# Attention with 16 queries and 2048 keys on one core: engine loops, whole V units, and a wait of QK on V

## The chip, the cores and the metric

The kernel runs on one core of a Trainium2 chip. The metric is device time in microseconds (us) of one execution. Executions of one kernel mostly agree within 0.1%, so differences of 1 us can be told apart here if enough runs stand beside each other.

## The reference

```
B, H, Sq, Skv, Dh = 8, 16, 16, 2048, 256        # q, k, v in bf16
scores = einsum('bhqd,bhkd->bhqk', q, k) * Dh ** -0.5
attn   = softmax(scores, axis=-1)
out    = einsum('bhqk,bhkd->bhqd', attn, v)
```

There are 128 heads. K and V are 134 MB each and every byte is used once, while a head has 16 queries only: the kernel is a stream of 268 MB from HBM with some arithmetic beside it.

## The kernel before

A *unit* is four heads: 8192 rows of K or V, laid out as 128 partitions x 64 rows x 256, so a partition's share of a unit is one contiguous run of 32 KB. A *block* g is the two units 2g (even) and 2g+1 (odd). There are 16 blocks. K and V each have one SBUF buffer for an even and one for an odd unit. A *packet* is one contiguous run that one of the 16 DMA engines moves: 32 KB when a unit is loaded whole, 16 KB when it comes in halves.

For a block, DVE transposes K in eight pieces (`kt`), PE multiplies (`qk`), DVE takes the maximum, ACT the exponential, DVE transposes P (`pt`, `px`), and PE multiplies by V (`pv`) one block later. A *hardware loop* lets an engine repeat one stretch of instructions for every block; an *unrolled* stream has every block written out. Only PE loops here. The parts:

```python
def v_parts(u):                                   # pieces in which a V unit is loaded
    return vparts.get(u, [HT, HT] if u % 2 else [NT])       # NT = 64 rows, HT = 32
# V of block g may be loaded when PV of block g-1 is done:
#   deps = ... [("pv", g - 1, 1)] if g else ...
# K of block g, unit e, when the last transpose of block g-1, unit e, is done: [("kt", g - 1, e, 3)]

for g in range(G):                                # order of the loads in SP's queue
    for u in (2 * g, 2 * g + 1): k_load(u)
    if g:
        for u in (2 * g - 2, 2 * g - 1): v_load(u)

def qk(g, e, h):
    j_qk[g, e, h] = J("pe", "qk", ..., [("kt", g, e, 2 * h + 1), ("qwb", g, e) if h == 0 else None,
                                        ("exp", g - 1, h) if g and e == 0 else None])
def pv(g, h):                                     # first half needs only half of the odd unit
    j_pv[g, h] = J("pe", "pv", ..., [("px", g, h), ...]
                   + (j_v[2 * g] + j_v[2 * g + 1][:1] if h == 0 else j_v[2 * g + 1][1:]))

qk_block(0)                                       # PE's order; a hardware loop over blocks on PE alone
for g in range(1, last):
    qk_block(g); pv(g - 1, 0); pv(g - 1, 1)
# ... cut: the last block, ACT's and DVE's orders (unrolled), stores on ACT's queue
```

## Time and profile before

The kernel before takes 640.6 us (median of 3 runs, 640.5 to 640.74). These are lines of its page. In the first part: engine, busy us, share of the span, instructions. In the 40 slices a digit is a tenth of busy time. In the DMA part: packets, MB, share of 16 engines.

```profile
span 639.2 us, 4824 instructions
PE 489.1 (77%) x2176; PEld 166.7 (26%) x1680; DVE 427.8 (67%) x372; ACT 99.1 (16%) x208; POOL 4.2 (1%) x7
PEclk9979979799897999899898998997979989899899
DMA  9999999999999999999999999999999999999996
...
q1 hardware_dynamic: 13488, 269.51, 98.7%
q10 hardware_dynamic: 2288, 1.03, 0.6%
q8 instruction: 4, 0.07, 0.0%
q14 instruction: 6, 0.05, 0.0%
```

DMA is full in 39 of 40 slices, and no compute engine is near that. q1 is SP's queue (loads), q10 ACT's (stores), and the two instruction queues fetch program code through the same DMA engines. The window view of one steady block, from one landing of even K to the next (length, busy time of each engine, granted clock, DMA share, GB/s):

```profile
233.63:272.69 39.06, 30.36 (x124) 9.53 (x93) 26.49 (x23) 5.66 (x12) 0.00 (x0) 0.91 1.01 431
```

The Trainium skill, "DMA: Bandwidth & Descriptors", section Specifications, gives 435 GB/s as the fabric ceiling. The 431 GB/s here lie just under it. The timeline of the kernel before around the even K that landed at 233.6 us (start, length, engine, line, operation):

```profile
218.98 13.97 PE L171 MATMUL O_ps<-VB,PT 128*128 128x512 bf16 x64 [1.27 <-DMA VB<-in_v_dram]
...
232.98 1.28 SPq L229 DMA_DIRECT2D VB<-in_v_dram  x3
...
233.63 8.89 DVE L126 STREAM_TRANSPOSE KB<-KN 128x2048 f32<-128x2048 f32 x4 [9.38 <-DMA KN<-in_k_dram]
```

I call the landing of even K on its slowest DMA engine T (233.60 here; DVE starts 0.03 us later). PV ends at T-0.6 and the next V loads are issued at once. The odd K ahead of them in the queue keeps the DMA engines busy until T+9.7 (its 4 MB last 9.7 us), so the issue has ample time. In 3 of 14 blocks PV starts at half clock (*cold*: its first seven or eight matmuls come every 427 ns instead of every 215), as in the block after this one, where it takes 15.66 us instead of 13.97:

```profile
258.14 15.66 PE L171 MATMUL O_ps<-VB,PT 128*128 128x512 bf16 x64 [2.11 <-DMA VB<-in_v_dram]
```

There V is issued at T+1.2 (273.83, with T at 272.67), still early.

### The profile page before, as it was taken

The page shows a single profiled execution, that of the slowest core. Times are in us where ns is not written, and L with a number is a line of the kernel's source. Part 1 is how long each engine was busy: PE and PEld are TensorE (multiplying, and loading weights), DVE is VectorE, ACT ScalarE, POOL GpSimd, SP SyncE. Part 2 cuts the span into 40 slices and gives each one's busy share as a digit, 9 for nine tenths or more (in the row PEclk, how much of TensorE's full clock was granted, in tenths as well). Part 3 has the DMA queues.
Part 4 walks back from the last instruction along what each step waited for, and adds up shares of the span by engine and source line. Part 5 has one row for each costly group of instructions (what it writes and reads, how often), then busy time and mean ns, then how long its engine had stood idle before and what let it go on. Part 6 is the DMA issues. An engine that isn't in the chain of part 4 may idle for free.

```text
span 639.2 us, 4824 instructions
## 1 busy us (share of the span) xinstructions
PE 489.1 (77%) x2176; PEld 166.7 (26%) x1680; DVE 427.8 (67%) x372; ACT 99.1 (16%) x208; POOL 4.2 (1%) x7
## 2 busy tenths in 40 slices
PE   0857879676896768868689686787967878676998
PEld 0111313123131221312214122131311313122287
DVE  4879386693857949387492965938669395693861
ACT  2121112030120301212011120211203012030010
POOL 2000000000000000000000000000000000000000
PEclk9979979799897999899898998997979989899899
DMA  9999999999999999999999999999999999999996
GB/s 322 428 431 426 432 433 441 435 427 428 421 438 429 431 429 429 437 439 425 437 414 443 431 429 431 425 430 433 437 441 425 432 417 440 429 429 430 421 427 258
DMA packets 15786, 270.65 MB, mean 423 GB/s; under 512 B 1824, under 2 KB 4128, under 8 KB 4640
## 3 DMA queue, kind: packets, MB, share of 16 engines
q1 hardware_dynamic: 13488, 269.51, 98.7%
q10 hardware_dynamic: 2288, 1.03, 0.6%
q8 instruction: 4, 0.07, 0.0%
q14 instruction: 6, 0.05, 0.0%
HBM read 269.48 MB, written 1.05 MB: 423 GB/s over the span
## 4 chain that ended last, share of the span: by engine, by line
DMA 67%; DVE 25%; PE 7%; issue 1%; SPq 0%; DVEq 0%
DMA KN<-in_k_dram 67%; DVE KB L126 23%; PE O_ps L177 4%; PE S_ps L143 1%; PE S_ps L131 1%; DVE negm L148 0%; DVE PC L157 0%; SPq L110 0%; DVE PT L163 0%; DVE O_fin L323 0%; DVE O_fin L313 0%; DVE rab L292 0%; DVE rinv L291 0%; DVEq L410 0%; DVE ltot L289 0%
## 5 line engine op out<-in xcount | busy, mean ns | idle before, releaser
L126 DVE STREAM_TRANSPOSE KB<-KN 128x2048 f32<-128x2048 f32 x128 | 284.6, 2281 | 159.7 <-DMA KN<-in_k_dram 139.3
L143 PE MATMUL S_ps<-KB,QW 128*128 128x512 bf16 x528 | 213.1, 413 | 125.2 <-DVE KB L126 125.2
L171 PE MATMUL O_ps<-VB,PT 128*128 128x512 bf16 x896 | 200.7, 386 | 22.2 <-DMA VB<-in_v_dram 22.2
L131 PE MATMUL S_ps<-KB,QW 128*128 128x512 bf16 x496 | 203.9, 411 | 0.0
L143 PEld LDWEIGHTS S_ps<-KB,QW 128*128 128x128 bf16 x528 | 54.0, 103 | 327.7 <-issue 239.4
L171 PEld LDWEIGHTS O_ps<-VB,PT 128*128 128x128 bf16 x896 | 87.9, 99 | 138.0 <-issue 38.6
L119 ACT ACTIVATE QW<-QT 32x128 bf16<-32x128 bf16 x128 | 53.9, 421 | 320.5 <-PE S_ps L131 312.8
L163 DVE COPY PT<-PC 32x1024 bf16<-32x1024 bf16 x128 | 53.3, 416 | 4.3 <-PE O_ps L177 2.6
L157 DVE STREAM_TRANSPOSE PC<-P_sb 128x1024 bf16<-128x1024 bf16 x32 | 37.9, 1223 | 19.8 <-ACT P_sb L152 19.8
L152 ACT ACTIVATE P_sb<-S_ps,negm 128x1024 bf16<-128x1024 f32 x32 | 35.4, 1110 | 36.3 <-DVE negm L148 26.7
L148 DVE TENSOR_REDUCE negm<-S_ps 128x1 f32<-128x2048 f32 x16 | 36.7, 2292 | 4.6 <-PE S_ps L131 4.1
L308 ACT ACTIVATE O_tmp<-O_ps,rab 128x256 f32<-128x256 f32 x15 | 7.1, 474 | 157.9 <-PE O_ps L171 157.1
L177 PE MATMUL O_ps<-KN,PT 128*128 128x256 bf16 x128 | 14.4, 273 | 0.0
L177 PE MATMUL O_ps<-VB,PT 128*128 128x256 bf16 x128 | 14.1, 273 | 0.1
L177 PEld LDWEIGHTS O_ps<-VB,PT 128*128 128x128 bf16 x128 | 12.4, 98 | 2.0 <-DVE PT L163 0.6
L177 PEld LDWEIGHTS O_ps<-KN,PT 128*128 128x128 bf16 x128 | 12.4, 98 | 1.8 <-DMA KN<-in_v_dram 0.3
L323 DVE TENSOR_SCALAR O_fin<-O_ps,rab 128x256 bf16<-128x256 f32 x2 | 1.0, 483 | 11.5 <-PE O_ps L177 11.5
L313 DVE SCALAR_TENSOR_TENSOR O_fin<-O_ps,rab,O_tmp 128x256 bf16<-128x256 f32 x15 | 6.7, 448 | 1.8 <-issue 1.8
L152 ACT ACTIVATION_READ_ACCUMULATOR P_sb<-S_ps,negm 128x1 f32 x32 | 6.3, 196 | 0.0
L113 DVE STREAM_TRANSPOSE QT<-VB 128x2048 f32<-128x2048 f32 x1 | 2.3, 2311 | 5.5 <-DMA VB<-in_q_dram 5.5
L292 DVE TENSOR_SCALAR rab<-mask,rinv 128x2 f32<-128x2 f32 x16 | 3.7, 228 | 0.6
L190 POOL MEMSET PT<- 128x4096 f32 x1 | 3.5, 3512 | 0.0
(11 smaller groups left out, 7.8 us busy)
## 6 DMA issues: line engine op xcount, KB each, us to landing
KN<-in_k_dram SPq DMA_DIRECT2D x28, 4096.0 KB, 30.1
VB<-in_v_dram SPq DMA_DIRECT2D x32, 2048.0 KB, 26.5
VB<-in_v_dram SPq DMA_DIRECT2D x14, 4096.0 KB, 20.0
KN<-in_k_dram SPq DMA_DIRECT2D x8, 2048.0 KB, 15.3
KN<-in_v_dram SPq DMA_DIRECT2D x2, 2048.0 KB, 27.6
KN<-in_v_dram SPq DMA_DIRECT2D x2, 1024.0 KB, 23.1
KN<-in_v_dram SPq DMA_DIRECT2D x3, 512.0 KB, 25.8
VB<-in_q_dram SPq DMA_DIRECT2D x4, 256.0 KB, 4.4
```

Source lines behind the costliest of these rows:

```text
L119: ins = eng.activation(ap_of(dv, dv.offset + 32 * a + e, [[256, 4], [128, 2], [2, 16]]), ap_of(sv, sv.offset + 2 * (2 * g + e), [[64, 4], ...
L126: return eng.transpose(KBf[:, c % R_KB].rearrange("p t i -> p (t i)"), KNf[:, e].rearrange("p t i -> p (t i)")[:, n * c:n * c + n])
L131: return eng.add_instruction(mybir.InstMatmult(start_tensor_calc=start, stop_tensor_calc=stop, ldweights=False, tile_size=(128, 128), tile ...
L143: ins = mm(S_ps[:, 2 * h + c, :], QW[:, e, bp, :], rhs, start=(e == 0 and bp == 0), stop=(e == 1 and bp == 7))
L148: return eng.tensor_reduce(out=negm[:, g:g + 1], in_=S_ps[:].rearrange("p c n -> p (c n)"), axis=AX.X, op=ALU.max, negate=True)
L152: return eng.activation(P_sb[:, 1024 * h:1024 * h + 1024], S_ps[:, 2 * h:2 * h + 2, :].rearrange("p c n -> p (c n)"), ACTF.Exp, bias=negm[ ...
L157: return eng.transpose(PC[:, h].rearrange("p t x -> p (t x)"), P_sb[:, 1024 * h:1024 * h + 1024])
L163: ins = eng.tensor_copy(PT[pr, 32 * h:32 * h + 32, pr], PC[pr, h])
L171: ins = eng.matmul(O_ps[:, 0, :], PT[:, t, :], rhs, start=(t == 0), stop=(t == NT - 1))
L177: ins = eng.matmul(O_ps[:, bank, 0:D], PT[:, t, :], buf[:, t, :], start=(t == 0), stop=(t == NT - 1))
L308: j_ea[g] = J("act", "ea", lambda eng: eng.activation(O_tmp[:], src, ACTF.Copy, scale=rab[:, g, 0:1]), [("pv", g, 1) if g < last - 1 else ...
L313: j_eb[g] = J("dve", "eb", lambda eng: eng.scalar_tensor_tensor(out=O_fin[:, g % 2, :], in0=src, scalar=rab[:, g, 1:2], in1=O_tmp[:], op0= ...
```

## The change

It has three parts. First, DVE and ACT run as hardware loops of one block as PE does, with semaphore waits cut to what is needed; with that come one exp of 2048 instead of two of 1024, slices by register on ACT, and stores issued from SP's queue. Second, every odd V unit of blocks 0 to 13 is loaded in one piece, runs of 32 KB instead of two of 16 KB; PV then waits for all of it. Third, QK of the odd unit waits until the even V unit of the block ahead of it has landed, so that PV follows QK closely. The core of the diff, with cuts:

```diff
-        vparts = {NU - 2: [32, 32], NU - 4: [32, 32], NU - 1: [16, 16, 8, 8, 8, 4, 2, 2]}
+        vparts = {NU - 4: [32, 32], NU - 3: [32, 32], NU - 2: [32, 32], NU - 1: [16, 16, 8, 8, 8, 4, 2, 2]}
         def v_parts(u):
-            return vparts.get(u, [HT, HT] if u % 2 else [NT])
+            return vparts.get(u, [NT])
...
         for g in range(G):
             for u in (2 * g, 2 * g + 1):
                 k_load(u)
+            if g >= 3:
+                store("sp", g - 3)
             if g:
                 for u in (2 * g - 2, 2 * g - 1):
                     v_load(u)
...
-                              [("kt", g, e, 2 * h + 1), ("qwb", g, e) if h == 0 else None,
-                               ("exp", g - 1, h) if g and e == 0 else None])
+                              [("kt", g, e, 2 * h + 1), ("qwb", g) if e == 0 and h == 0 else None,
+                               j_v[2 * g - 2][0] if 0 < g < last and e == 1 and h == 0 else None,
+                               ("exp", g - 1) if g and e == 0 else None])
...
-                           [("px", g, h), ("eb", g - 1) if g and h == 0 else None]
-                           + (j_v[2 * g] + j_v[2 * g + 1][:1] if h == 0 else j_v[2 * g + 1][1:]))
+                           [("px", g, h), ("eb", g - 1) if g and h == 0 else None] + j_v[2 * g] + j_v[2 * g + 1])
...
-        emit_stream(nc.scalar, "act")
-        emit_stream(nc.vector, "dve")
+        emit_stream(nc.scalar, "act", ACT_SLOT)
+        emit_stream(nc.vector, "dve", DVE_SLOT)
```

(The two last added lines make ACT's and DVE's streams loops; the code that builds the loops and plans their waits is cut.)

## The prediction

> **What bounds the kernel now.** The DMA engines. The slices on the page show DMA at 9 (90% or more) in 39 of 40 slices, 423 GB/s over the span. The Trainium skill, "DMA: Bandwidth & Descriptors", Specifications, gives a fabric ceiling of 435 GB/s; the table of windows shows 431 GB/s in every steady block of 39.07 us, so this trace agrees. Summed packet times in the trace are 635 us per engine out of a span of 639.2. Compute only has to keep the queue fed. In the chain of waits 67% is DMA of K; the rest is work that runs beside DMA.
>
> **What changes.**
> 1. Packets. In the trace a 16 KB packet takes 612 ns and a 32 KB packet 1214 ns, so two halves cost about 10 ns more than one whole. Fourteen odd V units drop 128 packets each: 14 x 128 x 10 ns / 16 engines = about 1.2 us off the DMA stream, semaphore packets included (estimate from those durations).
> 2. Instruction fetches. Ten instruction packets lie in the span (six of 8 KB, four of 16 KB); the 8 KB ones look like the unrolled DVE, ACT and SP programs. Each delays one engine, and a transfer ends with its slowest: the 16 landings of one load spread 0.4 us at 27 us, 1.9 us after the fetch at 36 us, 3.1 us after the one at 486 us. With DVE and ACT looping I expect fewer; 0.3 to 1.3 us less spread at the end. PE already loops with no fetch per turn; I expect none for the new loops.
> 3. Feed margin. PV now starts only when all of odd V has landed, not its half, so the V buffers come free later. Call the landing of even K T: V lands at T-9.7, PV takes 13.97 us warm (15.66 with a cold start), so the next V load is issued at T+4.4 to T+6.1, against T+1.1 before. The K load queued ahead of it runs to T+9.7. The margin shrinks from 8.6 us to about 4 to 5, still positive, so no DMA bubble. The new QK wait lets QK end near T-10, so PV follows at once and stays warm (the skill, "TensorE: Matmul & The Clock Gate", part 1: idle time throttles the clock; here the trace shows matmuls at 427 ns after idle, 216 otherwise).
> 4. Loop branches, register waits, one exp instead of two, slices by register on ACT, store through SP: a few us per block at most, on engines idle 10 us or more per block.
> 5. Tail. PV of block 13 ends nearer the last QK, so that QK should run warm and start the closing PV about 2 us earlier relative to T; but the last V piece lands at 635.93 and PE ends at 636.59, so only some 0.3 us is to be had.
>
> **Prediction.** 640.6 - 1.2 - 0.8 - 0.1 = 638.5 us, range 637.0 to 640.8. Faster by over 2%: 0.01; within 2%: 0.96; slower by over 2%: 0.03.
>
> **What would show it.** Right: packets of SP's queue fall from 13488 to about 11500 plus the stores; steady blocks take 38.98 us instead of 39.07; V issues come 3 to 5 us later in the block; PV in 13.97 us nearly always; DMA still 9 in all slices; fewer instruction packets. Wrong: DMA slices below 9 or steady GB/s under 431.
>
> **What would make it wrong.** Instruction fetches on every turn of the new loops, delaying one engine some 0.5 to 1 us each (up to +14 us); or a V issue so late that the slowest engine runs dry each block.

## The result, and the profile after

The changed kernel takes 639.57 us (median of 6 runs, 639.45 to 639.73); the kernel before, beside it, 640.75 (6 runs, 640.5 to 640.93). The ratio is 0.9982, with a 95% interval of 0.9969 to 0.9995: the mean of the runs of one over that of the other in the same rounds, so not quite the ratio of the medians. Executions over 1.5% slower than the fastest of the same kernel are left out of the means. The gain is 1.2 us, real and far below 2%. The lines of the page after:

```profile
span 638.1 us, 5071 instructions
PE 490.0 (77%) x2176; PEld 166.1 (26%) x1680; DVE 428.2 (67%) x371; ACT 93.8 (15%) x176; POOL 4.2 (1%) x7
PEclk9977987979889798997979979799797989979999
DMA  8999999999999999999999999999999999999996
...
q1 hardware_dynamic: 13344, 270.36, 99.2%
q10 hardware_dynamic: 416, 0.18, 0.1%
q8 instruction: 4, 0.07, 0.0%
q14 instruction: 2, 0.02, 0.0%
```

Busy times hardly moved. DMA is still full. There are four fewer 8 KB instruction packets (q14 from 6 to 2). Stores moved from q10 to q1. A steady block in the window view:

```profile
233.42:272.44 39.02, 29.85 (x130) 9.47 (x97) 26.53 (x23) 5.81 (x11) 0.00 (x0) 0.91 1.00 432
```

This block is 0.04 us shorter; the mean over 13 blocks, below, is 0.066 shorter. And the timeline around the even K that landed at 272.44:

```profile
262.85 13.97 PE L172 MATMUL O_ps<-VB,PT 128*128 128x512 bf16 x64 [1.14 <-DMA VB<-in_v_dram]
...
272.54 2.31 DVE L128 STREAM_TRANSPOSE KB<-KN 128x2048 f32<-128x2048 f32 x1 [3.43 <-DMA KN<-in_k_dram]
...
276.86 0.86 SPq L230 DMA_DIRECT2D VB<-in_v_dram  x2
```

PV starts when all of V has landed and is warm in each of its 14 steady blocks (13.97 us), and the next V loads are issued at T+4.4 instead of T-0.6. In all 14 blocks the trace has this issue between T+4.41 and T+4.58.

### The profile page after: what moved, and what is told of

The parts are those of the page before. It is cut to its first block, busy times and chain, and to the rows that moved or that the text cites. A ratio compares the mean times of both kernels' runs of the same rounds, so it can differ in the third digit from the quotient of the medians.

```text
span 638.1 us, 5071 instructions
## 1 busy us (share of the span) xinstructions
PE 490.0 (77%) x2176; PEld 166.1 (26%) x1680; DVE 428.2 (67%) x371; ACT 93.8 (15%) x176; POOL 4.2 (1%) x7
## 3 DMA queue, kind: packets, MB, share of 16 engines
q1 hardware_dynamic: 13344, 270.36, 99.2%
## 5 line engine op out<-in xcount | busy, mean ns | idle before, releaser
L145 PE MATMUL S_ps<-KB,QW 128*128 128x512 bf16 x528 | 217.0, 420 | 137.2 <-DMA VB<-in_v_dram 94.1
L133 PE MATMUL S_ps<-KB,QW 128*128 128x512 bf16 x496 | 207.7, 419 | 0.0
L172 PE MATMUL O_ps<-VB,PT 128*128 128x512 bf16 x896 | 195.6, 379 | 6.8 <-DMA VB<-in_v_dram 6.8
L154 ACT ACTIVATE P_sb<-S_ps,negm 128x2048 bf16<-128x2048 f32 x16 | 31.5, 1967 | 414.1 <-DVE negm L150 414.1
L122 ACT ACTIVATE QW<-QT 32x128 bf16 (+1 forms) x128 | 54.0, 422 | 11.2 <-DVE QT L113 9.9
L301 DVE COPY rab<-rab 128x2 f32<-128x2 f32 x15 | 2.5, 167 | 1.2
```

The source lines that it names most:

```text
L122: ins = eng.activation(ap_of(dv, dv.offset + 32 * a + e, [[256, 4], [128, 2], [2, 16]]), src.rearrange("p (s b) t -> p b t s", b=4), ACTF. ...
L133: return eng.add_instruction(mybir.InstMatmult(start_tensor_calc=start, stop_tensor_calc=stop, ldweights=False, tile_size=(128, 128), tile ...
L145: ins = mm(S_ps[:, 2 * h + c, :], QW[:, e, bp, :], rhs, start=(e == 0 and bp == 0), stop=(e == 1 and bp == 7))
L154: return eng.activation(P_sb[:], S_ps[:].rearrange("p c n -> p (c n)"), ACTF.Exp, bias=negm[:], scale=1.0, accum_out=lsum[:])
L172: ins = eng.matmul(O_ps[:, 0, :], PT[:, t, :], rhs, start=(t == 0), stop=(t == NT - 1))
```

## The experiments

Three questions: which part brings the 1.2 us, what the QK wait is for, and how much later V could be issued. Runs of one call shared a chip and the runs of the kernel before. A figure that recurs below, the *pace*, is the time from one landing of even K to the next on the first DMA engine to finish, averaged over 13 steady blocks of a trace: 39.066 us before, 39.000 after. The *spread* is the time between the first and the last of the 16 DMA engines that bring in one load.

### The loops alone

Odd V back in halves, PV waiting by halves, no QK wait; the loops stay. (Two lines that give the second half its own semaphore are cut.)

```diff
-            return vparts.get(u, [NT])
+            return vparts.get(u, [HT, HT] if u % 2 else [NT])
-                               j_v[2 * g - 2][0] if 0 < g < last and e == 1 and h == 0 else None,
-            ... + j_v[2 * g] + j_v[2 * g + 1])
+            ... + (j_v[2 * g] + j_v[2 * g + 1][:1] if h == 0 else j_v[2 * g + 1][1:]))
```

> The changed kernel with its loops, but odd V units in two halves again, PV waiting for the halves as before, and no QK wait on V. Theory (the DMA stream sets the time: packets, plus the lag of the slowest DMA engine): the steady block goes back to 39.07 us, instruction packets stay few (two of 8 KB in the span), the end spread of landings stays near 2.7 us instead of 3.1; time 0.1 to 0.6 us under the kernel before, so about 640.3. Rival (loops themselves cost or save time on the engines): steady block clearly away from 39.07 us, or time over 1 us from the kernel before.

Measured: 640.85 us (median of 6, 640.45 to 641.01) against a median of 640.65 for the kernel before. The pace is 39.063 us, as expected. The instruction packets fell to 6, as expected, and the spread at even K of block 15 fell with them, from 3.10 to 2.19 us. But by the last piece of V it was 2.92 us, against 3.09 before, and the last landing came at 635.99 us against 635.93. The expected small gain is not there. Nor does the end spread follow the loops: the unrolled kernels of the next section end with 2.83 and 2.73 us, the looped ones of this document with 2.7 to 3.1 where the queue did not run dry and no filler was added.

### V and the QK wait alone, on the unrolled kernel

The same edits in the other direction, on the kernel before: odd V whole, PV waits for all of it, QK waits for V.

> The kernel before, unrolled on DVE and ACT, with odd V whole and the QK wait on V. Theory: the steady block (pace of the first engine to land) is 39.01 us as in the changed kernel, about 0.7 us less over the span, but the six 8 KB instruction packets stay and the end spread stays near 3 us; time about 640.0. Rival (the loops brought the gain): time like the kernel before, 640.7.

> The kernel before with odd V whole and the QK wait, DVE and ACT unrolled, beside the changed kernel. What the loops are worth is the difference: 0.2 to 0.6 us above the changed kernel if four more 8 KB instruction packets (about 0.3 us each on one engine, more in its lag) reach the end; no difference if the lag is evened out in the tail.

Measured: 640.05 (639.32 to 640.54), and in the second call 639.98 (five runs: 639.77, 639.98, 641.33, 640.71, 639.54). The pace is 39.014 and 39.031. Under the kernel before that is 0.60 by the medians of the first call; in the second it is 0.81 by the medians and 0.47 by the means. So about half of the gain or somewhat more is here, without the loops. In the second call the mean is 640.27, which is 0.67 above the changed kernel beside it (639.60), with far more scatter. The traces show ten and eleven instruction packets (one of the eleven has 40 bytes) instead of six, and 19 and 31 packets of 32 KB that took over 1300 ns instead of 2 to 4. That goes with the difference; nothing here isolates it.

### The packets alone

The changed kernel with one thing undone: odd V units in two halves. PV still waits for all of V, QK still waits, the loops stay. (The second half's semaphore is cut here too.)

```diff
-            return vparts.get(u, [NT])
+            return vparts.get(u, [HT, HT] if u % 2 else [NT])
```

> The changed kernel with one thing undone: odd V units in two halves (PV still waits for all of V, QK still waits). Theory (packets alone): 14 x 128 packets more, 10 ns each over 16 engines: the steady block 39.06 us instead of 39.00, time 1.1 to 1.3 us above the changed kernel run beside it. Rival (the gain is in the order of PE's work): no change against it.

> The changed kernel again, to stand beside the other three of this call on one chip: 639.4 to 639.8 us, 1.0 to 1.3 under the kernel before.

Measured: changed kernel again 639.64 (mean 639.60, five runs from 639.34 to 639.69), in halves 640.75 (mean 640.74, 640.54 to 641.02), kernel before 640.79 (mean 640.74, nine runs). The SP queue of the run in halves:

```profile
q1 hardware_dynamic: 15360, 270.36, 99.2%
```

That is 2016 packets more than the changed kernel's 13344: 14 x 128 of data and 14 x 16 of the four bytes that report a landing. They cost 1.14 us. The pace is 39.089 us. With packets as before and everything else changed, the kernel takes what the kernel before takes, within 0.01 us. So in the changed kernel the packets carry the whole gain. It is not a plain sum, though: on the unrolled kernel the same packets brought 0.5 to 0.8 us, and the loops, worth nothing here, were worth 0.67 beside whole V units.

The packet times in the traces say the same more directly. Summed over the span and divided by 16, they are 635.1 us before, 635.3 in `halves_wait` and in `loops_only`, 633.7 and 633.8 in the two traces of the changed kernel, and 634.1 and 634.4 with whole V units on the unrolled kernel.

### Three more units whole

```diff
-            if g < 2:                     # K of blocks 0 and 1 in halves
+            if g < 1:
-        vparts = {NU - 4: [32, 32], NU - 3: [32, 32], ...
+        vparts = {NU - 3: [32, 32], ...
```

(The semaphore count of the K loads moves along.)

> The changed kernel with the three more units whole: both K units of block 1 and the first V unit of block 14 in 32 KB runs. Theory (packets set the time): 3 x 128 packets fewer, 10 ns each over 16 engines, 0.25 us less than the changed kernel: about 639.3. Rival: no change or slower, as these pieces are wanted early.

> The version with three more units whole, again, beside the changed kernel: 0.1 to 0.3 us under it if packets set the time, nothing if not.

Measured: 639.52 (639.07 to 639.58) in the first call, 639.49 (mean 639.40, 638.86 to 639.65) in the second, where the changed kernel had a mean of 639.60. The 0.2 us have the sign and size that were expected, but four of the five runs overlap with the changed kernel's. Both traces have 633.6 us of packet time per engine, 0.2 under the changed kernel. Call it the fastest version here by a hair; the times do not show it beyond noise.

### Without the QK wait

```diff
-                               j_v[2 * g - 2][0] if 0 < g < last and e == 1 and h == 0 else None,
```

> The changed kernel without the wait of odd QK on V. Theory: PE has spare time, so nothing changes: within 0.1% of the changed kernel (639.6), although QK ends earlier, some PV start cold (15.66 us instead of 13.97) and V loads are issued up to 1.7 us later in those blocks. Rival (PV close behind QK is what pays): slower than the changed kernel by 0.7 us or more.

Measured: 649.93 us (median of 7; 643.6 to 651.6), ten above the changed kernel's 639.57. My expectation fell and the rival held: the one line is worth more than eight times the gain of the whole change. The trace is of the fastest of these runs, 643.6 us. Its timeline around an even K that landed at 155.41:

```profile
145.82 16.75 PE L172 MATMUL O_ps<-VB,PT 128*128 128x512 bf16 x64 [7.03 <-DMA VB<-in_v_dram]
...
155.51 8.89 DVE L128 STREAM_TRANSPOSE KB<-KN 128x2048 f32<-128x2048 f32 x4 [9.08 <-DMA KN<-in_k_dram]
...
162.60 0.80 SPq L230 DMA_DIRECT2D VB<-in_v_dram  x2
```

PE had been idle for 7.03 us, so PV began at half clock and took 16.75 us instead of 13.97. V was issued at T+7.2. The window view from that landing to the next:

```profile
155.41:195.87 40.46, 30.96 (x137) 10.20 (x103) 26.54 (x23) 5.77 (x11) 0.00 (x0) 0.92 1.00 425
```

The block took 40.46 us and moved 425 GB/s. It is the longest of this trace; its pace is 39.31 us. The DMA queue had run dry: on the mean of the 16 engines 0.18 us of the block passed without a packet, and slow packets cost another 0.62 us (0.08 in the block of the changed kernel shown above). The DMA share still reads 1.00, since a packet that is slow counts as busy; the GB/s tell more. The page's busy share of PE is 75%, lower than the changed kernel's 77%. That share gives no hint that PE's timing is what costs.

### Warm by other means

The QK wait still missing; instead 28 matmuls whose result nobody uses keep PE busy until V lands.

```diff
+        def emit_fill(eng):
+            for i in range(28):
+                ins = eng.matmul(O_ps[:, 3, :], ident[:], QT[:, 0:512], start=True, stop=True)
+            return ins
             qk_block(g)
             if g:
+                J("pe", "fill", emit_fill)
                 pv(g - 1, 0)
```

> The changed kernel without the QK wait, but with 28 filler matmuls of 512 columns (about 6 us, their result unused) in the idle time of PE ahead of PV. Theory now (without the wait PV starts at half clock after 7 us idle and takes 15.3 to 16.8 us, so that V loads are issued too late and the DMA queue runs dry): PV back at 13.97 us, steady block back at 39.0 us, time 639.5 to 640.3, though PE has more work than in any kernel here. Rival (QK's place itself matters, whatever the clock): time stays at 643 us or more, as without the wait.

Measured: 639.82 us (five runs: 639.47, 639.76, 639.86, 642.07, 639.82). The clock row of its page:

```profile
PEclk9989999999999999999999999999999999999999
```

And a PV from its timeline:

```profile
263.25 13.97 PE L172 MATMUL O_ps<-VB,PT 128*128 128x512 bf16 x64 [0.96 <-DMA VB<-in_v_dram]
```

PE did more work than in any other kernel here, its mean clock rose from 0.909 to 0.995, and the ten microseconds were gone. So it is the clock at which PV starts that the QK wait buys; the place of QK does not matter in itself. One of five runs took 642.07 (mean clock 0.989, the others 0.992 to 0.995); it left no trace, so its cause is not known.

### V issued later on purpose

The changed kernel, with the V loads waiting also for the third (`late_v2`) or fourth (`late_v3`) transpose of the next block's even K.

```diff
-                deps = ... else [("pv", g - 1, 1)] if g else ...
+                deps = ... else [("pv", g - 1, 1), ("kt", g + 1, 0, 2)] if g else ...     # 3 in late_v3
```

> The changed kernel, V loads issued only after the third transpose of the next block's even K as well: about T+6.8 us instead of T+4.4 (T: landing of even K). Theory: from issue to data on the last DMA engine takes about 4 us, K ahead in the queue lasts to T+9.7, so the margin is some 1 to 1.5 us and 2.4 us of delay costs about 0.9 us a block: time 645 to 655. Rival (the margin of about 4 to 5 us that the prediction gave): no change, 639.6.

> As late_v2, after the fourth transpose: about T+9.0 us. Theory: another 2.2 us a block, all of it lost: 670 to 690 us. Rival (margin of 4 to 5 us): at most 645.

Measured: 654.3 us (4 runs, 653.05 to 656.17) with V at T+6.8, and 663.18 (4 runs, 662.41 to 663.37) with V at T+9.0. The first is as the theory had it, and rules out the margin of 4 to 5 us. The second costs far more than the rival allowed, but less than I expected: 8.9 us over the first, and under the 670 to 690 that I gave. I had taken about 4 us from issue to data. The issue of one block in the timeline of `late_v2`, where even K had landed at 236.53, and one of `late_v3`:

```profile
243.35 0.80 SPq L230 DMA_DIRECT2D VB<-in_v_dram  x2
...
249.18 0.80 SPq L230 DMA_DIRECT2D VB<-in_v_dram  x2
```

The trace of `late_v3` has no data packet in flight from 249.5 to 250.0, half of the engines at work by 250.25 and 15 by 250.5. From issue to data takes about 1.1 us when the engines are empty. What I had read as latency was partly slow packets. Splitting the loss in the four traces shows both. "Dry" is the time in which DMA engines had no packet, summed and divided by 16; "slow" is the time of 32 KB packets beyond their usual 1214 ns, summed and divided by 16:

```
               V issued at   dry     slow    both, over changed   profiled run   over changed
changed        T+4.4         0.03    1.18     0                   639.60          0
no QK wait     T+5.8 to 7.2  1.35    4.12     4.3                 643.60          4.0
late, third    T+6.8         5.26    8.71    12.8                 654.86         15.3
late, fourth   T+9.0        15.93    8.81    23.5                 663.37         23.8
```

The two terms account for the loss within 0.3 us in two rows. In the third row 1.6 of the missing 2.5 us lie in the spread of the last landing (4.3 us against 2.7). The slowest 32 KB packets of the three took 2.4, 2.8 and 2.4 us. A single packet as slow is nothing special (one took 3.1 us in the next experiment); it is their number: 144, 274 and 204 took over 1300 ns, against 31 at most in every other trace. In `late_v3` 199 of the 204 start between T+9 and T+11, so they are the first ones after the dry spell. Why they are slow is not shown.

### Instruction fetches in earnest

The changed kernel with PE's stream unrolled:

```diff
-            if name in turns:
+            if name in turns and name != "pe":
```

> The changed kernel with the PE stream unrolled, so that its instructions have to be fetched in every block: about 14 more instruction packets of 16 KB. Theory: each fetch delays one DMA engine by about 1 us; if always the same engine, the spread of landings grows to over 10 us and the time rises by up to 14 us; if they go round the engines, about 1 us per engine, time up by 0.5 to 2 us. Rival (instruction fetches do not matter to the time): within 0.3 us of the changed kernel, 639.6.

Measured: 640.35 us (640.2 to 640.46), 0.7 above the 639.6 of the changed kernel. Its instruction queues:

```profile
q8 instruction: 15, 0.25, 0.2%
...
q14 instruction: 2, 0.02, 0.0%
```

Eleven more packets of 16 KB, one for nearly each block. They go to different engines: the sorted lags of the 16 engines show a new one 0.6 to 1.6 us late with nearly each fetch. The spread at the end is 2.76 us, as in the changed kernel (2.68), while the mean landing of the last piece moved from 632.93 to 634.30 and its last landing from 634.86 to 635.45. The PE loop, which the kernel before has already, is thus worth about 0.7 us, as far as runs of different calls can be compared.

## Why the prediction was right, and where it was not

The total held: 638.5 us was predicted with a range of 637.0 to 640.8, and 639.57 came. That alone proves little, since the range holds the 640.6 of the kernel before too; of the 2.1 us that the sum promised, 1.2 came. Point by point:

- **What bounds the kernel: right.** DMA full in all slices but the first and last, 432 GB/s in the steady block shown. The pace is 39.00 us where 38.98 was predicted.
- **Step 1, packets: right, and with the loops in place it is the whole gain.** Predicted 1.2 us; undoing the packets alone costs 1.14 us. Two packets of 16 KB (612 ns each) take some 10 ns more than one of 32 KB (1214 ns). The count fell by 2016 as foretold, and the stores then joined the same queue, which is why the page shows 13344 instead of 11472 (the unrolled kernel with whole V has the latter).
- **Step 2, instruction fetches: the term that was mis-sized.** It stood in the sum with -0.8 us ("0.3 to 1.3 us less spread at the end"). Packets did fall, from ten to six, with no fetch per turn. But the spread at the end went only from 3.09 to 2.68 us (and to 2.83 and 2.73 without the loops), and with V in halves the loops give nothing at all (`halves_wait`: 640.74 against 640.74). The lag that I read off the landings at block 15 did shrink, by 1.0 us. What I overlooked are the fetches of PE's closing code, three of 16 KB after 590 us in both kernels: in the changed kernel they added 0.6 us to the spread, before none, as they met other engines. The largest lag is that of one engine, and nothing that I read foretells which one a fetch meets. The mean landing over the engines would not have been a better quantity: in the second trace of whole V on the unrolled kernel it is 633.71 us, before it is 633.73, and the times of these runs are 639.77 and 640.53.
- **Step 3, feed margin: right in what happens, wrong in the size and in what follows.** V is issued at T+4.4, PV takes 13.97 us, no bubble: all measured as predicted. (The T+1.1 that it gives for the kernel before is that of the three cold blocks; the other eleven have about T-0.6.) But I called T+6.1 equally safe and the margin "about 4 to 5". The prediction did say that the QK wait keeps PV warm; that its total never had to rest on the wrong margin is luck. Without the wait V comes at T+5.8 to T+7.2 (in the one trace) and the kernel loses 4 to 12 us; at T+6.8 in every block it loses 14.7. Beyond T+4.4 there is thus less than 2.4 us of room before a loss of that size. I had set the issue against the end of odd K on the slowest engine (T+9.7), and left out that the first engine ends 2.0 us earlier (T+7.7), that data follow an issue only after 1.1 us or more, and that the packets after a dry spell are slow.
- **The QK wait**, which I expected to make no difference when I took it out, is what makes whole V units affordable. Without it the same packets cost ten microseconds instead of saving one. The Trainium skill, "TensorE: Matmul & The Clock Gate", Part 1, describes the mechanism (an idle window of some 3.4 us halves the clock), and the trace agrees: after 7.03 us of idle time PV took 16.75 us, after 1.14 us 13.97 (the last section has a case between them). I had quoted that page and allowed for a cold PV of 15.66 us, 1.7 more than a warm one, but called its T+6.1 safe; after 7 us of idle time a cold PV costs up to 2.8 us.
- **Step 4, loop costs: right.** Nothing of registers, branches or the single exp shows in the time.
- **Step 5, tail: nothing came of it.** From the last landing to the end of the span it is 3.27 us where it was 3.25; -0.1 was predicted. The closing PV starts at T+21.1 after T+21.8, 0.7 us earlier instead of about 2, and in the second trace of the changed kernel 0.1 earlier.

Left open: why the runs without the QK wait scatter from 643.6 to 651.6 us (only the fastest left a trace; that it is where the idle time falls among the clock's windows is argued, not shown), and what makes the unrolled kernel with whole V 0.67 us slower and less steady than the looped one. The odd run of the kernel before, 649.84 us at a clock of 0.756, would fit a PV so slow that V came late; it left no trace either.

## What to carry to other kernels

In a kernel that DMA bounds, count packets times their fixed cost, and check for every load how long before the queue runs dry it is issued, on the first DMA engine to finish and with PE at its cold speed. An engine that is idle a quarter of the time can still set that moment: keep it warm before the work that frees a buffer, by moving work next to it or by filler. Test each line of a change alone even if the total came as predicted; here one part was worth ten microseconds, hidden behind a gain of one.

## What the Trainium skill lacked or had wrong

- "DMA: Bandwidth & Descriptors", section Bandwidth, says that for HBM to SBUF the HBM limit of about 358 GB/s binds. Here the program's one core reads 428 to 433 GB/s from HBM in the steady blocks before and after. The single-core table in the same section (425 GB/s at 16 MB) agrees; its note says that the other core of the pair was idle, a condition that the sentence on 358 GB/s leaves out.
- No page that I read says what a queue that ran dry costs besides the idle time: in the run with V after the third transpose 274 packets of 32 KB took over 1300 ns, the slowest 2.8 us instead of 1.21, and slow packets cost 7.5 us per engine more than in the changed kernel.
- "CRC Debugging", Comparing the Two Runs, puts the instruction refills on queue 14. Here PE's come on queue 8 in packets of 16 KB (4, and 15 with PE unrolled), while queue 14 has packets of 8 KB (6, and 2 with DVE and ACT in loops). No page tells that a refill puts one DMA engine 0.6 to 1.6 us behind in a full stream.
- "TensorE: Matmul & The Clock Gate", Part 1, advises against idle gaps over about 3.4 us. In the kernel before a gap of 2.1 us ahead of PV (256.03 to 258.14) already gave a cold start of 15.66 us, while one of 2.4 us (295.00 to 297.41) did not. The clock records of this trace start at 258.27, 316.30, 336.78, 493.79 us and so on, always a whole number of 3.413 us apart. On that grid the three gaps before a cold PV (2.0 to 2.6 us) each lie in one interval, and a boundary at 295.82 splits the gap of 2.4 us. So on the 14 gaps of this trace it counts where a gap falls, besides its length; gaps of up to 1.95 us in one interval left PV warm.
